# A recurrence followed by a two-layer network: the start rewritten as one hand-ordered list, with rows instead of broadcasts and matmuls on zeros

## The chip, the cores and the metric

The kernel runs on one core of one Trainium2 chip. The metric is device time in microseconds (us); a kernel's time is the median of its executions. A profile shows one of these executions. Its "span" runs from the first to the last instruction and is about 1.7 us shorter than the time of the same execution (203.68 against 202.0 us in the profiled execution of the kernel before). An execution that took over 1.5% more than the fastest of its kernel is called slow, the others fast; ratios use fast ones alone. PSUM is the memory that TensorE writes its results to. TensorE, VectorE, ScalarE and GpSimd are called PE, DVE, ACT and POOL in profile lines; PEld is TensorE's weight load; POOLq, SPq and so on are an engine's issuing of transfers.

## The reference, cut to what matters

```
# r, k, v: (4, 8, 768, 48) float32; w, u: (8, 48)
for t in range(S):
    cur = einsum('bhd,bhe->bhde', u[None] * kt, vt)
    y[:, :, t] = einsum('bhd,bhde->bhe', rt, state + cur)
    state = w[None, :, :, None] * state + einsum('bhd,bhe->bhde', kt, vt)
x = y.transpose(0, 2, 1, 3).reshape(B * S, H * D)      # 3072 x 384
h = x @ w_in                                           # 384 x 2048
out = (h * sigmoid(h)) @ w_out                         # 2048 x 384
```

The kernel cuts the 768 time steps into 6 chunks of 128. One chunk of one of the 4 batches is a unit; units 0 to 3 are chunk 0, units 4 to 7 chunk 1, and so on to 23. For each unit r and k are transposed on TensorE and multiplied by powers of w ("decay"); their product is masked and multiplied by v; the bonus, sum(r k u) v, is added; and for the next chunk a state is kept from k times powers of w ("decayed k") and v. Chunk n of y then feeds the two layers.

## The kernel before

All engines get their instructions in the order in which the program is written; there is no scheduler. What the change touches is the constants, two helpers, and the opening up to the loop. Cuts are marked with `# ...`.

```
nc.scalar.dma_start(out=u_bc, in_=...)     # u to all 128 partitions, 192 KB
nc.scalar.dma_start(out=w_bc, in_=...)     # w to all 128 partitions, 192 KB
for i in range(NIN):
    load(i)                                # r, k, v of units 0 to 3, all on SyncE's queue
# ...
def decayed_k(i):
    eng = nc.vector if i < B else nc.gpsimd
    eng.tensor_tensor(out=kc[...], in0=kin[...], in1=lamC, op=ALU.mult)
def bonus_v(i):
    nc.gpsimd.tensor_tensor(out=L(i)["vu"], in0=vin[i % NIN], in1=<sum, spread>, op=ALU.mult)
# ...
bonus_products(0); ld_win(0); turn(0); decay(0); cast_v(0); product(0); turn(1)
bonus_sum(0); bonus_v(0); masked(0); decayed_k(0); decay(1); bonus_products(1); ld_win(1)
outputs(0); evict_y(0); product(1); turn_y(0, True); state(0); load(4)
# ... units 2 to 5 in the same way, half blocks of chunk 0's first layer between them
fillers.extend([lambda ft=ft: l1(0, 2, 2, ft) for ft in range(8, NFT, 2)])
fillers.extend(second(0))
for i in range(B, NU, 2):                  # two units in one turn, from unit 4 on
    product_pair(i)
    for n in nxt: bonus_products(n); decayed_k(n)
    masked(i); masked(i + 1)
    fill(4)                                # matmuls of the two layers, as filling
    outputs(i); evict_y(i); turn_y(i, i < 6); state(i)
    # ...
```

`product_pair` is the products of two units together, 64 matmul instructions. A "half block" is a first-layer matmul group for 2 of the 4 batches of a chunk (6 instructions, 256 wide). In lists below, `A1` is the product of unit 1, `TR1` and `TK1` the transposes of its r and k, `ku1`, `ru1`, `rd1`, `vu1` its bonus (k u, then r times that, the sum, times v), `am1` its mask.

## Time and profile before

Three executions took 202.62, 202.63 and 203.02 us. The page has these totals; its lines, the stretches and the chain are shown in the prediction below.

| | busy us | share of the span of 202.0 us |
|---|---|---|
| TensorE | 183.1 | 91% |
| GpSimd | 117.3 | 58% |
| ScalarE | 107.8 | 53% |
| VectorE | 101.5 | 50% |

An engine that is busy 91% of the time is the bound in most stretches, but not in all: the slices show that its idle time lies at the start. The chain names the instructions that set the end, followed back from the last one.

### The profile page before, as it was taken

The numbers are of one execution on the slowest core, as the hardware profiler recorded it, in microseconds if no ns is written. First come the engines' busy times: TensorE is split into PE (matmuls) and PEld (weight loads), VectorE is DVE, ScalarE is ACT, GpSimd is POOL, SyncE is SP. The second block draws the span as 40 slices with busy tenths as digits, with TensorE's granted clock in tenths as the row PEclk, the third lists the DMA queues.
The fourth block names the chain that finished last, engine by engine and source line by source line (L and its number), as shares of the span: only waits on it lengthen the run. The fifth ranks groups of instructions, "written<-read, shape, count | busy, mean of one in ns | idle before, by whom it ended". The sixth has DMA issues, their size and how long they took to land.

```text
span 202.0 us, 5380 instructions
## 1 busy us (share of the span) xinstructions
PE 183.1 (91%) x2178; PEld 117.5 (58%) x2178; DVE 101.5 (50%) x175; ACT 107.8 (53%) x212; POOL 117.3 (58%) x151
## 2 busy tenths in 40 slices
PE   1675897996899999999999999999999999999993
PEld 0553785874566555675655665556665556644561
DVE  3686567374837266456464662672782464200121
ACT  4413478974306679128678057585066791179300
POOL 8686719998694983974956938918918530000000
PEclk9999999999789999999999999999999999999999
DMA  6899999991855907637629238459259101220022
GB/s 117 170 184 222 200 195 179 198 180 41 176 123 114 223 19 155 142 81 165 150 45 213 66 110 169 106 101 214 63 130 204 25 19 42 78 80 0 3 78 78
DMA packets 90265, 24.54 MB, mean 121 GB/s; under 512 B 83328, under 2 KB 90240, under 8 KB 90240
## 3 DMA queue, kind: packets, MB, share of 16 engines
q1 hardware_dynamic: 85824, 20.65, 47.2%
q0 software_dynamic: 3712, 3.15, 10.2%
q10 hardware_dynamic: 704, 0.40, 1.0%
q8 instruction: 17, 0.28, 0.6%
q14 instruction: 8, 0.07, 0.1%
HBM read 20.84 MB, written 4.72 MB: 127 GB/s over the span
## 4 chain that ended last, share of the span: by engine, by line
PE 84%; DVE 5%; DMA 3%; ACT 2%; SPq 2%; issue 1%; DVEq 0%
PE hps L335 32%; PE ops L347 31%; PE att L237 7%; PE att L204 5%; PE att L224 3%; PE yp L265 2%; SPq L74 2%; DVE rT L210 2%; PE yp L260 2%; DMA vin<-in_v_dram 2%; DMA rin<-in_r_dram 1%; DVE kT L210 1%; PE sp L275 1%; PE yT L323 1%; ACT xT L324 1%
## 5 line engine op out<-in xcount | busy, mean ns | idle before, releaser
L335 PE MATMUL hps<-xT,win 128*128 128x512 f16 (+1 forms) x336 | 68.2, 354 | 1.5 <-ACT xT L324 1.1
L347 PE MATMUL ops<-wout,gT 128*128 128x384 f16 x384 | 68.4, 332 | 0.0
L338 ACT ACTIVATE gT<-hps 128x512 f16<-128x512 f32 x96 | 55.4, 598 | 14.1 <-PE hps L335 11.6
L347 PEld LDWEIGHTS <-gT 128*128 128x128 f16 x384 | 36.7, 99 | 24.4 <-issue 1.7
L335 PEld LDWEIGHTS <-win 128*128 128x128 f16 x336 | 31.9, 100 | 28.3 <-issue 2.1
L181 POOL TENSOR_TENSOR vu<-vin,rku 128x384 f32<-128x384 f32 x24 | 19.8, 829 | 36.9 <-DVE rku L176 33.6
L244 DVE TENSOR_TENSOR am<-att,maskM 128x1024 f16<-128x1024 f32 x14 | 17.1, 1223 | 34.0 <-PE att L237 31.5
L352 ACT COPY osb<-ops 128x384 f32<-128x384 f32 x20 | 9.6, 479 | 45.3 <-PE ops L347 45.3
L165 POOL TENSOR_TENSOR ku<-kin,u_bc 128x384 f32<-128x384 f32 x24 | 24.1, 1004 | 3.8 <-DMA kin<-in_k_dram 1.9
L167 POOL TENSOR_TENSOR rku_f<-rin,ku 128x384 f32<-128x384 f32 x24 | 24.7, 1028 | 1.9
L210 DVE TENSOR_TENSOR rT<-att,lamR 112x512 f32<-112x512 f32 x24 | 16.5, 687 | 14.8 <-PE att L204 6.9
L288 DVE TENSOR_TENSOR y<-yp,vu 128x384 f16<-128x384 f32 x20 | 11.1, 557 | 18.0 <-PE yp L265 7.4
L171 POOL TENSOR_TENSOR kc<-kin,lamC 128x384 f16<-128x384 f32 x20 | 20.0, 1001 | 0.0
L237 PE MATMUL att<-rT,kT 48*64 48x64 f32 (+1 forms) x640 | 16.1, 247 | 1.8 <-DVE kT L210 1.8
L237 PEld LDWEIGHTS att<-rT,kT 48*64 48x64 f32 x640 | 14.5, 133 | 5.3 <-issue 3.2
L210 DVE TENSOR_TENSOR kT<-att,lamK 112x512 f32<-112x512 f32 x24 | 16.3, 680 | 0.0
L204 PE MATMUL att<-ident,rin 64*112 64x64 f32 x192 | 10.7, 235 | 5.6 <-DMA rin<-in_r_dram 3.7
L176 DVE TENSOR_REDUCE rku<-rku_f 128x8 f32<-128x384 f32 x24 | 12.3, 542 | 3.7 <-POOL rku_f L167 3.7
L204 PEld LDWEIGHTS att<-ident,rin 64*112 64x112 f32 x192 | 7.7, 139 | 10.3 <-POOL stb L128 3.7
L354 DVE COPY osb<-ops 128x384 f32<-128x384 f32 x4 | 2.2, 557 | 22.4 <-PE ops L347 22.4
L282 POOL TENSOR_TENSOR sdec<-st,wCT 112x384 f32<-112x384 f32 x16 | 13.2, 826 | 0.0
L217 ACT CAST rT<-rT 112x512 f16<-112x512 f32 x20 | 12.4, 623 | 0.1
(57 smaller groups left out, 173.6 us busy)
## 6 DMA issues: line engine op xcount, KB each, us to landing
rin<-in_r_dram SPq DMA_DIRECT2D x24, 192.0 KB, 3.7
kin<-in_k_dram SPq DMA_DIRECT2D x24, 192.0 KB, 3.7
vin<-in_v_dram SPq DMA_DIRECT2D x24, 192.0 KB, 3.6
out_dram<-osb SPq DMA_DIRECT2D x24, 192.0 KB, 2.1
win<-in_moe_w_in_dram POOLq DMA_DIRECT2D x4, 384.0 KB, 6.1
wout<-in_moe_w_out_dram POOLq DMA_DIRECT2D x4, 384.0 KB, 8.3
xT<-y SPq DMA_TRANSPOSE x18, 2.3
u_bc<-in_u_dram ACTq DMA_DIRECT2D x1, 192.0 KB, 5.1
```

Of the source, the lines that this page charges most:

```text
L165: nc.gpsimd.tensor_tensor(out=ku, in0=kin[n][:, :, 0:D], in1=u_bc, op=ALU.mult)
L167: nc.gpsimd.tensor_tensor(out=L(i)["rku_f"], in0=rin[n][:, :, 0:D], in1=ku, op=ALU.mult)
L171: eng.tensor_tensor(out=kc[i % NIN][:, :, 0:D], in0=kin[i % NIN][:, :, 0:D], in1=lamC, op=ALU.mult)
L181: nc.gpsimd.tensor_tensor(out=L(i)["vu"], in0=vin[i % NIN], in1=L(i)["rku"].unsqueeze(2).broadcast_to([128, H, D]), op=ALU.mult)
L204: nc.tensor.transpose(t[0:PR, y, x, p, :], flat[rows, 128 * p:128 * p + PR], ident[rows, rows])
L210: nc.vector.tensor_tensor(out=L(i)[key].rearrange("p g (y t) -> p y g t", y=2), in0=L(i)["t"][0:PR, :, x], in1=lam.rearrange("p g (y t) -> ...
L237: nc.tensor.matmul(a[e][o0:o0 + HC, j, p, c0:C], kT[r0:r0 + D, p, s0:s0 + HC], rT[r0:r0 + D, p, c0:C], start=True, stop=True)
L244: nc.vector.tensor_tensor(out=am.rearrange("p h g c -> p (h g) c"), in0=L(i)["a"].rearrange("p h g c -> p (h g) c"), in1=(maskX if crossed ...
L282: nc.gpsimd.tensor_tensor(out=L(i)["sdec"], in0=st[b], in1=wCT.unsqueeze(2).broadcast_to([PR, NP, PW]), op=ALU.mult)
L335: nc.tensor.matmul(hps[:, f, :], win[:, q, (ft + f) * 128:(ft + f + 1) * 128], xts[sc][:, q, b0:b0 + nb, :].rearrange("p b t -> p (b t)"), ...
L338: nc.scalar.activation(out=gts[sc][:, ft:ft + m, b0 * C:(b0 + nb) * C], in_=hps, func=AF.Silu)
L347: nc.tensor.matmul(ops, gts[sc][:, ft, b * C:(b + 1) * C], wout[:, ft, :], start=(ft == 0), stop=(ft == NFT - 1))
```

## The change

The intent is to start TensorE's steady work earlier: the r, k and v of chunk 0 go ahead of the big transfers, u and w arrive as single rows and are spread over the partitions by TensorE, some work changes engine, and units 0 to 5 with all half blocks of chunk 0 are put in one hand-made order. Matmuls on a tile of zeros are put into waits, to keep TensorE's clock up. The loop starts at unit 6 instead of 4.

```
-    nc.scalar.dma_start(out=u_bc, in_=...)               # broadcast, 192 KB
-    nc.scalar.dma_start(out=w_bc, in_=...)               # broadcast, 192 KB
+    nc.scalar.dma_start(out=u_row, in_=...)              # one row, 1.5 KB
+    nc.scalar.dma_start(out=w_row, in_=...)
+    for i in range(B):
+        for dst, src in ((rin, r), (kin, k), (vin, v)):
+            ld(i, dst, src, nc.scalar if i < 2 and dst is kin else nc.sync)
 # ...
+    def spin(ps_tile):                                   # matmuls on zeros
+        for _ in range(spins[0]):
+            nc.tensor.matmul(ps_tile, idle[:, 0:128], idle[:, 0:ps_tile.shape[-1]], ...)
+        spins[0] = 0
+    def spread_row(key, row):
+        spread[key] = ps.tile([128, HD], FP, ...)
+        nc.tensor.matmul(spread[key], ones, row, start=True, stop=True)
 # ...
     def decayed_k(i):
-        eng = nc.vector if i < B else nc.gpsimd
-        eng.tensor_tensor(...)
+        nc.gpsimd.tensor_tensor(...)
+    def bonus_v_rows(i):                                 # units 0 to 3
+        nc.vector.tensor_tensor(out=L(i)["vu"], ...)
 # ...
-    bonus_products(0)
-    # ... some 90 calls
+    order = """
+        lnw 5*TR0 eK lamK rT0 8*TK0 v160 ub kT0 A0 ubc i_q0 v161 wb am0 ku0 TR1 lnwb TK1 lamC
+        rT1 Y0 i_q1 kT1 ru0 lr4 4*A1 v162 i_q2 rd0 TR2 vu0 TK2 kc0 lk4 lv4 y160 am1 ku1 yT0 S0
+        xT0 st0 ru1 lr5 kT2 2*Y1 rT2 1*TR3 kc1 lk5 rd1 1*A2 vu1 lv5 ku2 S1 y161 st1 ru2 lr6 am2
+        # ... six lines
+        r167 yT4 yT5 G2.14 ru6 xT4 xT5 kc7 rd6 vu6 ku7 ru7 stb4 rd7 stb5 vu7 v167
+    """
+    fillers.extend([lambda ft=ft: l1(1, 0, 2, ft) for ft in range(0, NFT, 2)])   # half blocks
     fillers.extend(second(0))
-    for i in range(B, NU, 2):
+    for i in range(B + 2, NU, 2):
```

In the list `8*TK0` means eight matmuls on zeros in front of TK0, `ub` and `wb` the spreads of u and w, `i_q0` a weight piece's transfer.

## The prediction

> **What bounds the kernel now.** I began with the summary, the slices and the stretches of ten microseconds.
>
> ```profile
> PE 183.1 (91%) x2178; PEld 117.5 (58%) x2178; DVE 101.5 (50%) x175; ACT 107.8 (53%) x212; POOL 117.3 (58%) x151
> ...
> PE   1675897996899999999999999999999999999993
> ...
> PEclk9999999999789999999999999999999999999999
> DMA  6899999991855907637629238459259101220022
> ```
>
> ```profile
> 0.00:10.00 10.00, 3.61 (x36) 2.97 (x38) 4.96 (x19) 4.29 (x8) 7.28 (x22) 1.00 0.74 143
> 10.00:20.00 10.00, 6.48 (x75) 4.97 (x73) 7.42 (x10) 2.63 (x9) 7.62 (x9) 1.00 1.14 202
> 20.00:30.00 10.00, 9.24 (x94) 7.40 (x95) 5.72 (x10) 5.73 (x12) 4.22 (x5) 1.00 1.11 197
> ...
> 50.00:60.00 10.00, 8.73 (x121) 5.75 (x122) 6.11 (x11) 2.48 (x5) 7.74 (x10) 0.83 0.71 155
> 60.00:70.00 10.00, 10.00 (x139) 6.05 (x136) 5.33 (x10) 6.10 (x13) 7.09 (x10) 1.00 0.81 175
> ```
>
> (The columns are start:end, length, busy PE, PEld, DVE, ACT, POOL, clock, DMA share, GB/s.) From 60 us to the last copies TensorE is never idle but for one 0.37 us: that part is matmul work, and the change does not lighten it. Idle TensorE lies before 52 us, some 15 us of it, while the DMA engines are full until about 43 us. So the question is when the regular loop is entered. The chain that ended last, in order of time, shows a second loss:
>
> ```profile
> 13.60 2.08 PE att L224 x16
> ...
> 20.19 2.08 PE att L224 x16
> ...
> 23.27 2.72 PE hps L335 x12
> ...
> 26.58 1.42 PE hps L335 x12
> ...
> 28.37 1.09 PE att L224 x16
> ...
> 51.71 1.55 PE att L237 x56
> 53.26 4.39 PE ops L347 x16
> ...
> 62.39 2.71 PE ops L347 x16
> ```
>
> The same 16 product instructions take 2.08 us before 26 us and 1.09 after; the same 12 half-block matmuls 2.72, then 1.42. TensorE ran at half speed for the first 26 us, although the clock row says 1.00 there. At 53.26 sixteen matmuls took 4.39 us instead of 2.71: here the row does dip (0.83). TensorE had been nearly idle from 49.3 to 51.7.
>
> **What the Trainium skill says.** "TensorE: Matmul & The Clock Gate", Part 1, says the array starts at half clock, is released after about 3.4 us of sustained activity, and falls back after an idle window as long. The trace agrees in the factor (2.08/1.09, 2.72/1.42) and in the relapse at 53 us. This is what the matmuls on zeros are for. "DMA: Bandwidth & Descriptors", Issuing engines are not separate DMA queues, says that issuing from several engines saves only issue time, since all share 16 DMA engines; so moving two k loads to ScalarE buys order, not bandwidth. This trace has the engines full at about 200 GB/s; it does not test the claim. "GPSIMD Engine Reference", 4.1 Engine selection, calls GpSimd about 2x slower for two-input elementwise work. Here the v product is 829 ns on POOL and a like-sized add on DVE 557, a factor of 1.5. "ScalarE: Activation LUTs", What ACT_TABLE_LOAD costs, gives 1283 ns for a load; the trace has 1283 too, in front of the first silu at 24.74 us.
>
> **The change part by part.**
> *Removed.* The broadcast loads of u and w (2 x 192 KB): at 143 to 202 GB/s about 2 us of DMA in the first 10 us. They become 1.5 KB rows and two TensorE spreads. The exponent table for r leaves DVE (0.69 us); four short exps with a scale replace it and the 0.63 us exp. Four POOL v products (0.83 each) go to DVE, at an estimated 0.56; four decayed-k products come from DVE (0.66 to 1.39) to POOL at 1.00. POOL's sum stays nearly the same.
> *Moved.* The first weight piece is now issued ahead of the bonus products, so at about 4.5 us instead of 9.2; the silu table load sits behind the decay powers, in ACT idle time. Units 0 to 5 are interleaved by hand with all 16 half blocks of chunk 0, and units 6 and 7 are transposed before the loop. The loop starts at unit 6.
> *Added.* 24 zero matmuls, in front of waits; at the doubled rate some 4 us, nearly all idle anyway. Chunk 1's first layer in half blocks: 96 matmuls at 0.114 (24 in 2.73 us) against 48 at 0.216 (48 in 10.36): +0.55 us.
>
> *Until the first half block.* rin0 lands at 3.7 us in the trace, and is issued 0.5 later now: 4.2. kin0 goes behind three small loads on ScalarE's queue: I take 5.8. Transpose, 0.69 decay, then product 0 at 7.3 (7.68 before), say 1.6 us half warmed; its mask (1.22) ends near 10. k of unit 1 lands near 9.5; rT, kT (0.69 each) follow, so product 1 runs 11.1 to 12.2. The bonus sum (0.54), v product (0.56), eviction (0.55) and mask 1 (1.22) then take DVE to about 15. Product 2 waits for rT2 and, being queued behind r of unit 3's transpose, for that load: ten row tiles (1.97 MB) and about 0.8 MB of weights; the trace had moved 2.38 MB at 15.2 and 3.5 MB at 20.2, so about 17. Product (1.1), state product, ScalarE's four state copies (1.1) and the xT copy (0.48) give the first half block at about 20.5 (23.27 before, cold).
>
> *From there to the pair product of units 6 and 7.* TensorE work at warm times: 16 half blocks at 0.71 = 11.4; product 3, 1.1; nine half transposes at 0.26 = 2.4; pair product 4/5, 1.5; three outputs, 1.1; four state products, 0.9; four y transposes, 1.2. Sum 19.6 us. Before, TensorE was idle 12% of 25 to 50 us (21.96 busy of 25). I take the same 12%, because nothing has slack: in the stretch ACT has 16 silus (9.6), five xT copies (2.4), state copies (2.2), four r casts (2.5), five v casts (2.5) and four vx copies (2.0) = 21.2 us; DVE about 17.5; and POOL, from its first bonus product at 8.3, has 24 products at 1.0, eight at 0.83, two casts and seven weight issues at 0.8, thus is booked to 45.7. 19.6/0.88 = 22.3, so the pair product starts at 42.8. Before, that was 51.71: 8.9 us earlier.
>
> *The rest.* When before reached this point it had done four second-layer parts (16 matmuls, 2.6 us) that after still owes. The clock relapse (4.39 - 2.71 = 1.7) and the 0.37 wait at 122 us should go. ScalarE is likely behind with xT of units 4 and 5, which the loop's first half blocks need: 0.5.
> Sum: -8.9 + 2.6 + 0.55 - 1.7 - 0.4 + 0.5 = -7.3 us, and 202.63 - 7.3 = 195.3.
>
> **The rivals.**
> *ScalarE or POOL becomes the bound.* 21.2 of 22.3 us on ACT in fixed order, with four PSUM buffers shared by half blocks, outputs, states and transposes: one late state copy stops TensorE. If ACT runs at 85%, the stretch takes 25 us, and the time is 198. Against it: half blocks take 0.71 on TensorE, silus only 0.60.
> *The loads are the bound anyway.* Until unit 7 is in, 24 row tiles, four w_in pieces and one w_out piece must land, 6.7 MB; the trace had moved that by 37 us. The last transposes come near 40, so it just fits. If the weights now crowd out the rows, product 2 slips to 19 and more: 197 to 198.
> *The clock stays cold.* If zero matmuls with gaps, and transposes, do not lift it until 20 us, products 0 to 2 cost 1 us more each, and the half blocks start about 3 us later: 198.
> *Better than I think.* The order looks tuned against the chip: with no idle TensorE in the stretch the pair comes at 40 and the time is 192.5.
>
> **Range and chances.** The errors that I can name lie within about 3 us below and 3 above, and few together reach zero gain: the debt of 2.6 is certain, the 8.9 is not. Range 191.5 to 198.8. Two per cent faster is 198.6. Chances: faster 0.88, within 2% 0.10, slower 0.02.
>
> **What would show it.** In the changed profile: the 16 instructions of product 1 at about 1.1 us, not 2.08 (clock); the first half block at 20 to 21 us, without a table load behind it; the first pair product after unit 5's at 42.8; no dip in the clock row near 53; the loop with TensorE at 10 of 10 us. It is wrong if idle TensorE between 20 and 43 us is much over 12%, with ACT or POOL as releaser; if the r load of unit 3 arrives after 18; or if the loop shows new waits because POOL is behind at its entry.

## The result, and the profile after

Four executions of the changed kernel took 200.25 to 201.08 us, median 200.88; the kernel before, in the same rounds, 202.64. The ratio is 0.9904, with a 95% interval of 0.9878 to 0.9929: within 2%, and outside the predicted range of 191.5 to 198.8. (A ratio here is the mean time of one kernel's fast runs over that of the other's in the same rounds, so not quite the ratio of the medians.)

First, from the page of the kernel after, the same four lines as of the kernel before, and the shares of the chain.

```profile
PE 188.1 (95%) x2254; PEld 122.4 (61%) x2254; DVE 102.6 (52%) x176; ACT 107.9 (54%) x216; POOL 117.7 (59%) x151
...
PE   5899798989799999999999999999999999999992
...
PEclk9999999999999999999999999999999999999999
DMA  5999999899149258279175386291395102310022
...
PE 76%; POOL 16%; issue 4%; DVE 1%; ACT 1%; POOLq 0%; DVEq 0%
```

TensorE is now busy from the first slice, and the dip of the clock row is gone. Yet busy time rose by 5.0 us while the span fell by 3.0: part of the filled idle time is filled with something that was not there before. And 16% of the chain runs over GpSimd, which the chain of before does not name.

The stretches of ten microseconds, with the columns of the prediction's second fence:

```profile
0.00:10.00 10.00, 6.88 (x31) 3.15 (x31) 4.49 (x18) 3.80 (x8) 4.66 (x20) 1.00 0.90 168
10.00:20.00 10.00, 9.99 (x97) 6.43 (x96) 5.96 (x8) 5.50 (x13) 8.42 (x9) 1.00 1.10 192
20.00:30.00 10.00, 8.50 (x100) 6.09 (x100) 8.82 (x13) 5.89 (x17) 9.38 (x11) 1.00 1.04 198
...
50.00:60.00 10.00, 8.62 (x114) 6.69 (x112) 8.11 (x15) 6.35 (x12) 9.00 (x13) 1.00 0.30 58
60.00:70.00 10.00, 10.00 (x143) 6.86 (x141) 4.74 (x9) 1.96 (x4) 9.46 (x11) 1.00 0.65 157
```

From 10 to 20 us TensorE is busy 9.99 of 10 us (6.48 before), with 97 instructions against 75: 3.5 us more busy time for 22 more instructions. And from 50 to 60 it is idle for 1.4 us, at the loop's entry. After that it is full, as before.

The chain in order of time (start, duration, engine, tile, line, number of instructions) says what the busy time at the start is, and what happens at the entry:

```profile
6.11 1.86 PE att L151 x8
7.98 0.61 PE att L249 x8
8.58 1.57 PE bc L172 x2
10.16 2.01 PE att L279 x16
12.17 1.58 PE bc L172 x2
...
49.53 1.01 POOL rku_f L203
...
50.56 0.55 DVE rku L218
51.11 1.14 DVE am L299
...
52.30 0.22 PE yp L315 x2
...
71.55 5.35 PE hps L397 x48
...
100.08 5.29 PE hps L397 x24
```

L151 is the zeros, L172 the spreads, L279 a product. Of the 7.6 us from 6.11 to 13.75, 5.0 are zeros and spreads. At 49.53 GpSimd makes r k u of unit 7, on which VectorE's sum waits, and behind the sum stand the masks that TensorE waits for. The two last lines price a half-block detail: 48 instructions of half width take 5.35 us, 24 of full width 5.29.

Single instructions, from the timeline of the kernel after (start, us, engine, what; in brackets the idle time of that engine before it and its releaser):

```profile
16.84 1.46 PE L279 MATMUL att<-rT,kT 48*128 48x128 f32 x16
...
24.68 0.82 PE L397 MATMUL hps<-xT,win 128*128 128x256 f16 x6
...
46.17 1.98 PE L292 MATMUL att<-rT,kT 48*64 48x128 f32 x64
...
50.56 0.55 DVE L218 TENSOR_REDUCE rku<-rku_f 128x8 f32<-128x384 f32 x1 [3.23 <-POOL rku_f L203]
...
52.30 0.22 PE L315 MATMUL yp<-v,am 128*128 128x48 f16 x2 [1.38 <-DVE am L299]
```

Product 1 starts at 16.84 (the prediction: 11.1), the first half block at 24.68 (20.5; 23.27 before, though cold there), the pair product of units 6 and 7 at 46.17 (42.8), and at 52.30 TensorE has waited 1.38 us for a mask. At this point three causes for the missing 5.6 us offered themselves, and the experiments were made to tell them apart: matmuls that the change itself put into TensorE's queue, at half clock (zeros, spreads; theory A in the expectations below); one position in VectorE's order at the loop's entry; and GpSimd as a bound, since its share of the chain went up so much (theory B). A fourth, that the loads crowd each other out (theory C), is asked by bringing the broadcasts back.

### The profile page after: what moved, and what is told of

Same layout as the page of the kernel before. It is cut to its first block, busy times and chain, and to the rows that moved or that the text cites. A ratio compares the mean times of both kernels' runs of the same rounds, so it can differ in the third digit from the quotient of the medians.

```text
span 199.0 us, 5520 instructions
## 1 busy us (share of the span) xinstructions
PE 188.1 (95%) x2254; PEld 122.4 (61%) x2254; DVE 102.6 (52%) x176; ACT 107.9 (54%) x216; POOL 117.7 (59%) x151
## 4 chain that ended last, share of the span: by engine, by line
PE 76%; POOL 16%; issue 4%; DVE 1%; ACT 1%; POOLq 0%; DVEq 0%
PE ops L418 32%; PE hps L397 25%; PE att L292 6%; PE att L249 5%; POOL kc L207 4%; POOL ku L199 4%; POOL rku_f L203 2%; PE yp L315 2%; POOL sdec L338 2%; PE yp L310 2%; PE bc L172 2%; POOL wout L89 2%; PE sp L327 1%; PE att L279 1%; PE att L151 1%
## 5 line engine op out<-in xcount | busy, mean ns | idle before, releaser
L397 PE MATMUL hps<-xT,win 128*128 128x256 f16 (+1 forms) x384 | 66.9, 326 | 0.4 <-ACT xT L385 0.4
L418 PE MATMUL ops<-wout,gT 128*128 128x384 f16 x384 | 65.8, 326 | 0.0
L418 PEld LDWEIGHTS <-gT 128*128 128x128 f16 x384 | 36.2, 98 | 23.1
L397 PEld LDWEIGHTS <-win 128*128 128x128 f16 x384 | 35.8, 98 | 23.0 <-issue 0.4
L223 POOL TENSOR_TENSOR vu<-vin,rku 128x384 f32<-128x384 f32 x20 | 16.5, 830 | 28.8 <-DVE rku L218 22.2
L207 POOL TENSOR_TENSOR kc<-kin,lamC 128x384 f16<-128x384 f32 x24 | 24.0, 1003 | 0.7 <-ACT wCT L180 0.7
L343 DVE TENSOR_TENSOR y<-yp,vu 128x384 f16<-128x384 f32 x24 | 13.3, 556 | 13.1 <-POOL ku L199 4.7
L315 PEld LDWEIGHTS <-am 128*128 128x128 f16 x192 | 9.7, 98 | 4.8 <-DVE am L299 3.2
L299 DVE TENSOR_TENSOR am<-att,maskX 128x1024 f16<-128x1024 f32 x10 | 12.1, 1214 | 0.0
```

What stands on the lines that cost most here:

```text
L207: nc.gpsimd.tensor_tensor(out=kc[i % NIN][:, :, 0:D], in0=kin[i % NIN][:, :, 0:D], in1=lamC, op=ALU.mult)
L299: nc.vector.tensor_tensor(out=am.rearrange("p h g c -> p (h g) c"), in0=L(i)["a"].rearrange("p h g c -> p (h g) c"), in1=(maskX if crossed ...
L315: nc.tensor.matmul(L(i)["y"][:, h, :], L(i)["am"][:, j, p, :], L(i)["vy"][:, h, :], start=not sc, stop=(not sc or j == 1))
L397: nc.tensor.matmul(hps[:, f, :], win[:, q, (ft + f) * 128:(ft + f + 1) * 128], xts[sc][:, q, b0:b0 + nb, :].rearrange("p b t -> p (b t)"), ...
L418: nc.tensor.matmul(opss[b], gts[sc][:, ft, b * C:(b + 1) * C], wout[:, ft, :], start=(ft == 0), stop=(ft == NFT - 1))
```

## The experiments

All kernels gave correct results. Timed ones ran five rounds against the kernel before. An interval in brackets is the 95% interval of the ratio. In the first call the kernel before had a median of 202.98 us (27 executions), in the second 202.77, in the third 202.87. In the second call some executions, of both kinds of kernel, took 300 to over 1000 us; they are classed slow, are in no number below, and are not explained here.

### e1: no matmuls on zeros

```
-            spins[0] = int(n)
+            spins[0] = 0
```

> All 24 zero matmuls of the changed kernel taken out, all else kept. Theory A (TensorE instructions that the change itself put in order before products 0 and 1, run at half speed, delay the start): transpose of k of unit 0 starts about 1 us sooner than its 7.9 us, product 0 at about 9.2; but the clock then comes up only after the dense half blocks begin, so products 1 and 2 take 2.08 us each and the first half blocks 2.7 us per 12: 0.5 to 1.5 us slower in all, 201.5 to 202.5. Theory B (GpSimd's booked order sets the time once it has begun; TensorE's speed hardly matters): GpSimd begins 0.9 us sooner, so the time falls to about 200.0. Theory C (the loads of rows set the start): no change, 200.9.

Measured: 200.50 us (199.63 to 201.16), ratio 0.9883 [0.9847, 0.9919]. This is about the time with all 24 zeros. The timeline shows why neither side wins:

```profile
23.43 1.46 PE L397 MATMUL hps<-xT,win 128*128 128x256 f16 x6
```

The first half block comes at 23.43 instead of 24.68, but takes 1.46 us instead of 0.82: in this execution the clock is low again by then, and the clock row dips to 0.83 from 20 to 30 us. So zeros are worth something, and cost something. Two things differ from what was expected: product 2 was not cold (1.21 us), and the fall is not in every execution. By their mean clocks four of the six have one (0.982 to 0.991) and two have none (0.998); these two took no less (200.68 and 201.02 us).

### e2: zeros only where TensorE would idle

The eight zeros ahead of TK0 and the four ahead of product 1 go, the others stay.

```
-        lnw 5*TR0 eK lamK rT0 8*TK0 v160 ub kT0 A0 ...
-        rT1 Y0 i_q1 kT1 ru0 lr4 4*A1 v162 ...
+        lnw 5*TR0 eK lamK rT0 TK0 v160 ub kT0 A0 ...
+        rT1 Y0 i_q1 kT1 ru0 lr4 A1 v162 ...
```

> Only the 8 zero matmuls before the transpose of k of unit 0 and the 4 before product 1 taken out. Theory A: product 0 about 0.9 us sooner (near 9.2 us), product 1 another 0.7 us sooner; if the clock still comes up by 20 us, 199.5 to 200.0. Theory B: GpSimd's first bonus product at 9.9 instead of 10.8, time 200.0. Theory C: no change, 200.9; k of unit 0 then still makes the transpose wait until nearly 7.9.

Measured: 199.52 us (199.23 to 199.74), ratio 0.9834 [0.9801, 0.9867]. In the timeline:

```profile
6.20 0.68 PE L249 MATMUL att<-ident,kin 64*112 64x64 f32 x8 [1.06 <-DMA kin<-in_k_dram]
...
22.95 0.81 PE L397 MATMUL hps<-xT,win 128*128 128x256 f16 x6
```

TK0 starts at 6.20 instead of 7.91, when its load lands. It writes the same PSUM tile that VectorE reads for rT0, and so could not start before rT0 is done either (in e9, where k comes sooner, it waits for that). The same holds for the eight zeros in front of it: in the changed kernel they could start only when rT0 was done (6.11), took 1.86 us at half clock, and outlasted the wait that they were meant to fill: k landed 4.6 us after its issue at 2.27, so at 6.9, and TK0 ran 1.0 us later. In e12 k landed at 6.5, and in e4 at 6.0, before the zeros began. The half block comes at 22.95, and is warm. The zeros that stay are the five at the very start and those ahead of Y1, TR3, A2 and Y2. Since the clock was up at product 2 without any zeros as well (e1), the later ones are likely what keeps it up; the two groups were not tested apart. Between e1 and e2 lies 1.0 us.

### e3: u and w by broadcast again

The spreads go, and each broadcast is issued behind one of the two k loads on ScalarE's queue.

```
-    nc.scalar.dma_start(out=u_row, ...); nc.scalar.dma_start(out=w_row, ...)
+        if i < 2:        # behind the loads of unit i
+            nc.scalar.dma_start(out=(u_bc, w_bc)[i], ...)
-        ... v160 ub kT0 A0 ubc i_q0 v161 wb am0 ku0 ...
+        ... v160 kT0 A0 ubc i_q0 v161 am0 ku0 ...
```

> u and w loaded broadcast over the partitions as in the kernel before (each behind one k load on ScalarE's queue), and the two TensorE spreads with their fp32 passes taken out. Theory A: product 0 at about 9.4 instead of 10.1, transposes of unit 1 about 2.3 us sooner than 13.7; time 199 to 199.5. Theory B: GpSimd's first bonus product starts when u has landed, near 8.3 instead of 10.8, and its whole order moves forward by about 2 us: 199.0. Theory C: 0.4 MB more ahead of the rows of units 1 to 3, which land up to 2 us later; no gain or a loss, 201 to 202.

Measured: 202.3 us in the median of the 18 fast executions (201.28 to 203.74; four slow ones took 204.6 to 206.1), ratio 0.9975 [0.9955, 0.9994]: slower than the changed kernel, although TensorE has two spreads (3.1 us) less to do. From the timeline:

```profile
17.93 0.51 ACT L230 CAST v<-vin 128x384 f16<-128x384 f32 x1 [9.41 <-DMA vin<-in_v_dram]
```

v of unit 1 was issued at 3.19 and landed 14.7 us later. GpSimd, which has u earlier in this run (7.11 instead of 10.76), issues its weight pieces at 8.06 and 9.83 instead of 11.72 and 13.48, and r of unit 2, waited for until 19.41, is late as well. The decay powers stand behind that cast on ScalarE, so GpSimd waited 8.97 us for them, and the first half block came at 26.77. The late spread of u in the changed kernel thus also held the weights back. What is shown is the late loads; that the weights made them late was asked in e7. The run also changed something else: ScalarE issued the broadcast of w only at 4.90, its first work (the logarithm of w), next in its order, ran at 5.34 instead of 3.45, and product 0 came at 11.03 instead of 10.09.

### e4: the bonus sum of unit 7 behind the masks

```
-        ... ku7 ru7 stb4 rd7 stb5 vu7 v167
+        ... ku7 ru7 stb4 stb5 v167
 # in the loop
+        if i == B + 2:
+            masked(i)
+            masked(i + 1)
+            bonus_sum(7)
+            bonus_v(7)
```

(The two masks move ahead of the next units' bonus products in program order for this one turn; they are on other engines.)

> Bonus sum of unit 7 moved behind the two masks of units 6 and 7 in VectorE's order (before it stood ahead of them and waited for GpSimd until 50.56 us); all else kept. If that order alone makes the 1.4 us wait of the outputs of unit 6 at the loop entry: mask of unit 6 at about 48, no such wait, 199.4 to 199.7. Theory B in its strong form (GpSimd is behind by itself): the wait only moves to the eviction of unit 7 or later, and the time stays within 0.3 us of 200.9.

Measured: 199.52 us (198.79 to 199.96), ratio 0.9827 [0.9794, 0.986]. The timeline of VectorE, and the chain's shares:

```profile
47.89 1.23 DVE L299 TENSOR_TENSOR am<-att,maskM 128x1024 f16<-128x1024 f32 x1 [0.86 <-PE att L292]
...
50.27 0.55 DVE L218 TENSOR_REDUCE rku<-rku_f 128x8 f32<-128x384 f32 x1
```

```profile
PE 86%; DVE 7%; ACT 2%; DMA 2%; issue 1%; SPq 0%; DVEq 0%
```

The mask is made at 47.89 instead of 51.03, as soon as the product is there; TensorE's wait of 1.38 us is gone, and no wait takes its place from 46 to 60 us. GpSimd makes the same products as in the changed kernel, and has left the chain altogether. Its 16% was the way to one wait, not a measure of how much it bounds.

### e5: e2 and e4 together

> The 12 zero matmuls of e2 taken out and the late bonus sum of e4, together. If they are two separate losses (start, and loop entry), the gains of 1.4 us each add up: 198.1, ratio to before near 0.976. If both only shifted the same GpSimd chain, the second adds nothing: 199.5.

Measured: the fast runs took 197.43 to 198.70 us (four, mean 198.2), ratio 0.9764 [0.9724, 0.9803]. From 0.9890 (the changed kernel, see e12) e2 takes 0.0056 and e4 0.0063, which makes 0.9771: within the intervals the two add up. They are two separate losses.

### e6: e5, and the spread of w behind the transposes of unit 1

```
-        ... i_q0 v161 wb am0 ku0 TR1 lnwb TK1 lamC
-        ... TK2 kc0 lk4 lv4 y160 am1 ku1 yT0 S0
+        ... i_q0 v161 am0 ku0 TR1 TK1 wb lnwb lamC
+        ... TK2 ku1 kc0 lk4 lv4 y160 am1 yT0 S0
```

(The second line moves GpSimd's bonus product of unit 1 ahead, so that it can go on while it waits for the powers of w. The two parts were not tested apart.)

> As e5, and TensorE's fp32 spread of w (1.6 us at half speed) put behind both transposes of unit 1 in its order; GpSimd takes the bonus product of unit 1 ahead of decayed k of unit 0. Theory A: transposes of unit 1 start at about 10.5 instead of 12, product 1 about 1 us sooner (VectorE has the mask between), time 0.5 to 1 us under e5. Theory B: decayed k of unit 0 comes about 1 us later, GpSimd ends no sooner, and the time stays within 0.3 us of e5. Theory C (r and k of unit 1 have only just landed): transposes still wait, on a load, no gain.

Measured: fast runs 197.04 to 197.42 us (five, mean 197.3), ratio 0.9718 [0.9693, 0.9742]: 0.9 us better than e5 in the same rounds (the two intervals just overlap, but each of these five is below each of the four of e5), and more than 2% faster than the kernel before. Its profiled execution was a slow one, so no time is read from that trace; e9 holds the same order, and its transposes of unit 1 start at 10.65 instead of 12.45 in e5.

### e7: e3 with the weights issued later

```
-        rT1 Y0 i_q1 kT1 ru0 lr4 4*A1 v162 i_q2 rd0 ...
-        xT0 st0 ru1 lr5 ... kc1 lk5 ...
+        rT1 Y0 kT1 ru0 lr4 4*A1 v162 rd0 ...
+        xT0 st0 ru1 i_q1 lr5 ... kc1 i_q2 lk5 ...
```

> As e3 (u and w broadcast by DMA, no spreads, all zero matmuls kept), but the second and third piece of w_in issued behind the bonus products of unit 1 and decayed k of unit 1 in GpSimd's order. Theory C for e3 (weights issued at 8 and 10 us crowded out the rows: r of unit 2 was waited for until 19.4 us): r of unit 2 lands near 13 and the time falls from 202.4 to 199 to 200. If the rows come late because of the broadcast loads themselves, the time stays at 202.

Measured: 201.5 us in the median of the 18 fast executions (199.82 to 202.73; four slow ones took 203.1 to 204.1), ratio 0.9925 [0.9899, 0.9951]. It wins back 1.0 us of the loss of e3, and in its trace r of unit 2 is transposed at 18.65 without a wait, and the first half block comes at 25.11 instead of 26.77. So the weights were part of what delayed the rows. But the fast executions lie in two groups, 199.8 to 200.6 and 201.4 to 202.7, and only one execution, of the slower group, has a trace. Its ratio is no better than that of the changed kernel (0.9890 and 0.9904), and the intervals overlap, so whether rows or broadcasts are better in this order is not settled. Half shown, half open.

### e8 and e11: decayed k of chunk 0 back on VectorE

```
     def decayed_k(i):
-        nc.gpsimd.tensor_tensor(...)
+        eng = nc.vector if i < B else nc.gpsimd
+        eng.tensor_tensor(...)
```

If GpSimd were a bound, taking four products (4 us) off it should help.

> The changed kernel with decayed k of units 0 to 3 back on VectorE, as in the kernel before; all else kept. Theory B (GpSimd's booked work is the bound to 50 us): GpSimd's last bonus product of unit 7 ends 3 to 4 us sooner, the loop entry's wait goes, 199.0 to 199.5. Theory A: VectorE (8.8 of 10 us busy from 20 to 30) becomes the new brake, masks come up to 1 us later each, time within 0.5 us of 200.9.

Measured in e8: 203.20 us (fast runs 203.05 to 203.36), ratio 1.0015 [0.9993, 1.0037]; its profile fell in a slow execution. So the same kernel was looked at once more.

> One look at the same kernel as e8 (decayed k of units 0 to 3 on VectorE), since its profiled execution was a disturbed one; e8's undisturbed times were 203.2. Expected: VectorE waits for decayed k's powers (ready near 15 us) ahead of the eviction of unit 0, so its order slips, and first half blocks near 27 instead of 24.7 us; GpSimd is not the last releaser before the loop any more.

Measured: 203.20 us in its one execution. The first half block came at 25.37 and the pair product at 48.63 (24.68 and 46.17 in the changed kernel), TensorE waited 1.1 us for decayed k, and the sum of unit 7 waited for GpSimd as long as ever, only later:

```profile
53.03 0.55 DVE L219 TENSOR_REDUCE rku<-rku_f 128x8 f32<-128x384 f32 x1 [3.24 <-POOL rku_f L203]
```

The four products took 0.54 to 1.90 us each on VectorE, ahead of evictions, sums and decays. Both expectations were missed: no theory gave a time as long as 203.2, and GpSimd was still the last releaser before the loop. Relieving GpSimd of 4 us made the kernel slower by 1.0015 - 0.9890, some 2.5 us. So GpSimd's sum of work is not the bound, and once the v products are on VectorE, moving decayed k away from it is a part without which nothing would have been gained. The allotment of the kernel before (decayed k on VectorE, v products on GpSimd) was not tried in the new order.

### e9: e6, and k of unit 0 issued first

```
+    ld(0, kin, k, nc.scalar)      # ahead of the rows of u and w
```

> As e6, with k of unit 0 issued on ScalarE's queue ahead of the rows of u and w (about 1.4 us instead of 2.3). Theory A and the load part of the start: k lands about 0.8 us sooner (transpose waited for it until 6.2 to 6.7 us in the runs without the zeros), product 0 at about 8.1, and the time falls by 0.5 to 0.8 against e6, to 196.7. Theory B: GpSimd waits for u through the spread, which still comes right after that transpose, so it gains the same 0.8; no difference expected between A and B here. If the bandwidth and not the place in the queue sets the landing, no gain: 197.4.

Measured: fast runs 197.13 to 197.49 us (five, mean 197.3), ratio 0.9718 [0.9694, 0.9743]: nothing gained over e6. r of unit 0 now landed later and its transpose ran at 5.08 (4.58 in the changed kernel), so the wait moved from one load to the other. The trace is the good one to read the best order from:

```profile
13.65 2.08 PE L281 MATMUL att<-rT,kT 48*128 48x128 f32 x16
...
22.36 0.82 PE L399 MATMUL hps<-xT,win 128*128 128x256 f16 x6 [0.21 <-ACT xT L387]
```

Product 1 starts 3.2 us earlier than in the changed kernel, yet at half clock in full (2.08 us), and the half block comes 2.3 us earlier.

### e10: e9 with two zeros ahead of product 1

```
-        rT1 Y0 i_q1 kT1 ru0 lr4 A1 ...
+        rT1 Y0 i_q1 kT1 ru0 lr4 2*A1 ...
```

> As e9, with two zero matmuls put back before product 1, which then waits 0.9 us for kT anyway. If zeros in a true wait help the clock up: product 1 takes 1.1 to 1.5 us instead of 2.08 and the time falls by 0.3 to 0.8 against e9. If the clock's rise is set by the work from 4 us on, or zeros delay what follows: within 0.2 us of e9, or slower.

Measured: 197.87 us (197.32 to 198.66), ratio 0.9748 [0.9718, 0.9777], an interval that overlaps that of e9. In the trace the zeros took 1.03 us from 13.45 and moved product 1 to 14.41, where it still took 2.08 us; the half block came at 23.43. In this execution (198.29 us) they did not lift the clock, and delayed what stood behind them. Three of the six took 197.3 to 197.5, as in e9, so nothing was gained, and a loss is not clear.

### e12: the changed kernel again

> The changed kernel itself, unchanged, in the rounds of these runs, so that the gains of e9 and e10 are taken on one chip: 200.9, ratio to before 0.990; spread of single times about 0.8 us, as a zero matmul run catches the clock at different moments.

Measured: 200.92 us (200.25 to 201.40), ratio 0.9890 [0.9863, 0.9916]. The result stands, and so does the wait at the entry (1.39 us). In this execution product 1 took 2.08 us instead of 1.46, so when the clock rises varies from one execution to the next.

## Why the prediction was wrong

The direction was right, and so were large parts: the stretch of work, TensorE full from 60 us, no dip of the clock near 53. The size was wrong: -7.3 us predicted, -1.8 measured. The working can be put beside the profiled execution term by term. It applied its differences, read from a profiled execution of 203.68 us, to the median of 202.63; from 203.68 they give 196.3, and the profiled execution of the changed kernel took 200.7.

| term | predicted | measured | difference, us |
|---|---|---|---|
| first half block | 20.5 | 24.68 | +4.2 |
| from there to the pair product | 22.3 | 46.17 - 24.68 = 21.5 | -0.8 |
| from there to the end of the span | 202.0 - 51.71 + 2.6 + 0.55 - 1.7 - 0.4 + 0.5 = 151.8 | 199.0 - 46.17 = 152.8 | +1.0 |
| base: profiled execution against the medians | 0 | 203.68 - 202.63 + 200.88 - 200.74 | +1.2 |
| sum | | | +5.6 |

**Step "Until the first half block": failed, and most of the miss.** Product 0 was put at 7.3 and came at 10.09; product 1 was put at 11.1 and came at 16.84. Product 2 was to wait for a load until 17 and came at 21.13; in the trace TensorE waited for no load between 4 and 25 us. The prediction followed loads and VectorE through this part, and gave "24 zero matmuls, in front of waits; at the doubled rate some 4 us, nearly all idle anyway", and the spreads no time at all. In the trace the 24 took 8.2 us. The eight ahead of TK0 took 1.86, the four ahead of product 1 took 1.88, each spread 1.57, all at half clock and all in TensorE's fixed order ahead of what was needed. An instruction placed "in a wait" is free only if it can start when the wait starts and ends before it does; the eight could not start until rT0 was read, and ended 1.0 us or more after k had landed. Shown: leaving those twelve zeros out takes the ratio from 0.9890 (e12) to 0.9834 (e2), some 1.1 us (two calls, each against the kernel before), and moving the spread of w, with one product of GpSimd, another 0.9 us (e5 to e6). With both, the first half block comes at 22.36 (e9), so experiments account for 2.3 of the 4.2 us. The spread of u, which also stands ahead of product 0, was not moved by itself; without it product 0 waited 0.86 us for kT0 instead (e3), so an estimate of its cost is 1.57 - 0.86 = 0.7 us.

**Its clock.** Product 0 was taken as 1.6 us and product 1 as 1.1. Product 0 took 2.08 in every trace of an undisturbed execution. Product 1, starting at nearly the same time in three looks at the same opening, took 1.46 (the changed kernel), 2.08 (e12) and 1.16 (e4, whose edit lies far behind it); wherever it ran before 16 us (e1, e2, e5, e9, e10) it took 2.08. The packed traces settle why: they hold the clock's records, of which the views show only a mean, and 1.00 where there is no record yet. The first record is the rise to full clock. It stands at 25.97 us in the kernel before, at 17.49 in the changed kernel, 19.73 in e12, 16.72 in e4, 18.13 in e2, 18.15 in e9, 19.71 in e10, and at 19.54 in e1, which has no zeros at all. So the rise comes earlier than in the kernel before, but no run here shows that the zeros bring it forward. Its moment differs between executions of one opening by up to 3 us, and within a trace the changes lie whole multiples of 3.413 us apart (in e1 3.413, 3.413 and 174.08).

The rival "the clock stays cold" was thus partly true: of the 4.2 us the clock accounts for some 0.5 on product 0 and 0.4 on product 1. That its "about 3 us later" lies near the 4.2 is luck. What the zeros are good for is later: the half blocks from 23 us on are warm with a few zeros before them (e2), and cold without in the traced execution (e1). One reading of the prediction was also too strong: it took the relapse at 53 us for agreement with an idle window of 3.4 us. TensorE's only waits in the last 3.4 us before that fall (at 53.27) were parts of two of 1.01 and 0.76 us, with four product instructions between them; before the fall in e1 (at 22.95) there was one of 1.08 and the beginning of one of 0.79.

**Step "From there to the pair product": held.** 19.6 us of work at 12% idle gave 22.3; it took 21.5 (19.8 of work, 8% idle). The rival of ScalarE or GpSimd as bound did not come true here: TensorE's idle time from 24.68 us to the pair product comes to 1.7 us in all. One term of VectorE was mis-sized, here and in the step before (two of the four lie in each): the v products were estimated at 0.56 us. The groups of the changed kernel say otherwise, with the like of them on GpSimd above:

```profile
L223 POOL TENSOR_TENSOR vu<-vin,rku 128x384 f32<-128x384 f32 x20 | 16.5, 830 | 28.8 <-DVE rku L218 22.2 <-DMA rin<-in_r_dram 6.6
...
L212 DVE TENSOR_TENSOR vu<-vin,rku 128x384 f32<-128x384 f32 x4 | 4.7, 1170 | 0.1
```

They took 1170 ns on average, more than the 830 on GpSimd. Whether any of it lay on the path was not tested by itself.

**Step "The rest": right terms, one missing.** The debt of four second-layer parts is real. Half blocks of chunk 1 were mis-sized: 48 instructions of half width cost 0.06 us more than 24 of full width, so 96 cost 0.12 and not 0.55. ScalarE was not behind with xT (0.5 predicted; no such wait at the entry). The missing term is the 1.38 us for the mask. The prediction warned of "new waits because POOL is behind at its entry" but counted nothing for it, and it booked GpSimd to 45.7 from a start at 8.3; it started at 10.76, because u came through the spread, and its v product of unit 7 ended at 52.2 (51.38 + 0.83). Even that would have cost nothing had the sum of unit 7 not stood ahead of the masks in VectorE's order (e4: 1.3 us by the ratios). The order of instructions was there to be read before the run. The pair product took 1.98 us from its start, 0.43 more than the 1.55 that the prediction read. That is no slower product: it began before kT of unit 7 was ready (46.54) and stood waiting inside, and the 1.55 covers only the part from 51.71, behind such a wait; four instructions had run at 50.51. Together: 1.38 + 0.43 - 0.43 - 0.5 = 0.9 of the 1.0.

**The base.** "The clock relapse (4.39 - 2.71 = 1.7) ... should go" took a saving from something that the median does not contain. Of 70 later fast executions of the kernel before, in all three calls, 8 have a mean clock of 0.988 or 0.992, like the profiled one, and take 203.01 to 203.99 us (mean 203.6); the other 62 have 1.0 and take 201.46 to 204.26 (mean 202.8). The saving could be had only in executions like those 8, and is nearer to 0.9 us than to 1.7.

**"POOL's sum stays nearly the same"**, and the sum of the prediction has no term for the exchange of engines. The sum did stay (117.3 and 117.7 us), but the half of the exchange that takes decayed k off VectorE is worth some 2.5 us (e8). What it relieves is VectorE's order and no engine's sum: this is argued from the waits in e11, not shown by itself.

As a check on the account: with the entry wait gone and the half block at 22.36 (e9), 1.9 us instead of 4.2 late, the table's sum becomes 5.6 - 2.3 - 1.3 = 2.0, so 197.3; e9 measured 197.3. What keeps even the best order from 195.3 is, by its own trace, the first half block (1.9 late) and the base (1.2), less some 1.0 gained behind the half block. Of the 1.9, products 0 and 1 at 2.08 us instead of 1.6 and 1.1 make 1.5 by arithmetic; no run tested that.

**What stays open:** which work makes the clock rise in the first 20 us; what the spread of u costs; the two groups of times in e7 and in e10. In both, mean clocks just below 1.0 (0.996 to 0.999) go with the faster group: five of 7 against one of 11 in e7, three of 3 against none of 3 in e10. Where a trace shows such a mean (the changed kernel, e5, e11), it comes from a fall after TensorE's last matmul, so the groups may differ in how the clock's steps lie against the kernel's start; no trace of the faster groups was kept. The slow executions of the second call are open too.

e6 and e9 beat both kernels: 197.3 us, ratio 0.9718.

## What to carry to other kernels

Work put into a wait has to be checked like any other: what must be done before it can start (the buffer it writes counts), how long it takes at the clock of that moment, and what is queued behind it on the same in-order engine. When an engine's share of the chain jumps, look for the one instruction through which the chain enters it, and try its position in the consumer's order before moving work. Before subtracting a loss seen in one profiled execution, see whether the median contains it.

## What the Trainium skill lacked or had wrong

- "TensorE: Matmul & The Clock Gate", Part 1, puts the rise of the clock after about 3.4 us of sustained activity. Here TensorE was busy almost without a gap from 6.11 us, and the record of the rise stands at 17.49 (19.73 in the second look at the same kernel). The page does not say what kind of matmul counts as activity; these were transposes, one-row spreads, fp32 products and zeros. Its view that the moment differs between executions agrees, and so does its window of 3413 ns: the changes within a trace lie whole multiples of 3.413 us apart. Its idle window before a fall, read as 3.4 us without work, does not agree: before a fall TensorE had waited only 1.01 and 0.76 us (the kernel before), and 1.08 and at most 0.79 us (e1).
- "GPSIMD Engine Reference", 8. Key points, says that GpSimd and VectorE contend when VectorE reads two inputs from SBUF; the section gives no size. Here a v product of 128x384 fp32 on VectorE took 0.78 to 1.50 us in the changed kernel and 0.56 to 1.87 in e9, and on average it was slower there than on GpSimd (1170 ns against 830). That contention is the cause was not tested.
- No page gives the cost of spreading a 384-wide fp32 row over 128 partitions by TensorE: two matmul instructions, 1.57 us at half clock. Nor a figure for how far a 192 KB load can be put back by others issued near it: 14.7 us from issue to landing in e3, against a median of 5.1 for the v loads of the first 20 us in the changed kernel.
- The clock row of the profile shows 1.00 in the stretches in which the products took 2.08 us: no page says that such a row has nothing to show before the clock's first record.
